# The first batch's keys arrive with the sequence along the free axis, and every engine's list is ordered anew

## The chip, the cores and the metric

The kernel runs on one core of a Trainium2 chip. The metric is the device time of one execution in microseconds (us). A core has five engines that each work through a list of their own: TensorE (PE: matmuls, with PEld for the loading of weights), VectorE (DVE), ScalarE (ACT), GpSimd (POOL) and SyncE (SP), which here issues every DMA. They wait for one another by semaphores. The shapes are fixed: batch 8, 8 heads, sequence 576, head dimension 64; 4608 tokens of width 512 and an FFN of width 2048.

## The reference

```
q_s = exp(q - max(q, over the 64 of a head));  q_s /= sum(q_s) + 1e-9
k_s = exp(k - max(k, over the 576 of the sequence));  k_s /= sum(k_s) + 1e-9
kv  = k_s^T v            (64 x 64 for each batch and head)
x   = q_s kv             -> tokens (4608) x model (512)
h   = x w_in;  g = h * sigmoid(1.702 h);  out = g w_out
```

The softmax of the queries runs along the head dimension, that of the keys along the sequence. All is fp32.

## The kernel before

Tokens are taken in 12 blocks t of 384 (128 partitions x 3). The work falls into a start (attention of the first blocks while the weights stream in), the FFN of blocks 0 and 1 straight from the freshly converted weights, and the FFN of the other ten blocks by a scheme of sums and products of quarter matrices (lines 1251, 1386 and 1514). The change touches the start.

**Keys of one batch** (`k_max` and `k_sub`, two groups i of four heads). `load_k` brings a group as 128 partitions x 4 heads x 5 chunks x 64: the partition is the position in the sequence, so the maximum over the sequence goes across chunks and partitions. VectorE takes maxima over chunks (lines 581, 584, 587), GpSimd reduces across the 128 partitions (line 591), VectorE subtracts the maximum (line 605), ScalarE takes the exponential of 1280 elements per partition (line 610). The last chunk has only 64 positions of its own; it is filled up with repeated ones, whose V rows count nothing through a zero in V's column of ones, which gives the sum.

**KV and x.** `kv_pairs` multiplies K by V for two pairs of heads (line 643, 40 short matmuls), VectorE divides by the sum (lines 651, 652, 661). The queries go through `q_soft` (lines 711 to 731), are transposed by TensorE (`q_tr`, line 753, three transposes for a pair of heads) and copied out by ScalarE (line 760). `x_pairs` multiplies them by KV (line 825), and `x_out` splits x into a high and a low half: ScalarE copies the high one (line 789), TensorE subtracts it in PSUM (line 799), ScalarE copies the rest (line 801).

**Weights.** `w_in` and `w_out` come as 64-bit words, wi and wo with a number j from 0 to 15 for a slice of 128 of the FFN's width; from 2 on two slices come together. `conv_w` turns them into a high and a low fp32r half in five steps: c1 on ScalarE (line 448), c2, a shift (line 452), and c3, a combination (line 456), on VectorE, c5, the cast to the high half, on ScalarE (line 463), c6, the low half, on VectorE (line 473).

**FFN of a block.** `g1` is 12 matmuls of 384 columns (line 853) with x and wi[j], then the activation and its two halves; `g2` three pieces of three matmuls of 512 columns (line 885) with wo[j].

**Dummy groups.** `warm` (line 1599) multiplies the identity by itself twice into a bank that nothing reads; a group shows as four matmuls in the trace. Ten groups are in the lists before.

**What sets the order.** Every step is added to a `Plan` with its engine, a cost, and what it reads and writes. Which step comes when is then fixed by the list FIRST: FIRST[n] is the place of the n-th step. A step starts on its engine only behind the step of that engine with the next lower place, so FIRST gives each engine its list; costs and ranks in the code no longer change it.

Of the kernel before, what the change touches and what calls it, by code (L numbers as in the profile page):

```python
# [11 lines left out]
U32 = mybir.dt.uint32  # L12
AF = mybir.ActivationFunctionType
# [4 lines left out]
class Plan:  # L18
# [95 lines left out]
LIMIT = 48  # L114
FIRST = [
# [177 lines left out]


@with_exitstack
def efficient_attention_then_gelu_ffn(
    ctx: ExitStack,
    tc: tile.TileContext,
    q: bass.AP,
    k: bass.AP,  # L300
    v: bass.AP,
    w_in: bass.AP,
    w_out: bass.AP,
    eye: bass.AP,
    out: bass.AP,
# [226 lines left out]
    def load_q(t, i, rank):  # L532
# [32 lines left out]
        )  # L565

    nm = [0]
    maxes, made = {}, {}

    def k_max(b, i, rank):  # L570
        n = group(b)
# [1287 lines left out]
```

## Time and profile before

| | us |
|---|---|
| median of 3 runs (lowest, highest) | 826.06 (825.77, 826.37) |
| the profiled execution | 825.61 |
| its span, first to last instruction | 823.8 |
| TensorE busy (share) | 807.6 (98%) |
| VectorE busy | 607.9 (74%) |
| ScalarE busy | 488.7 (59%) |
| GpSimd busy | 24.0 (3%) |

The span is measured between the first and the last instruction; the execution's own time has 1.8 us around it. A matmul's duration in the trace includes the time in which it runs through the array, so that successive ones overlap; the distance between their starts says what one costs.

### The profile page before, as it was taken

The page shows a single profiled execution, that of the slowest core. Times are in us where ns is not written, and L with a number is a line of the kernel's source. Part 1 is how long each engine was busy: PE and PEld are TensorE (multiplying, and loading weights), DVE is VectorE, ACT ScalarE, POOL GpSimd, SP SyncE. Part 2 cuts the span into 40 slices and gives each one's busy share as a digit, 9 for nine tenths or more (in the row PEclk, how much of TensorE's full clock was granted, in tenths as well). Part 3 has the DMA queues.
Part 4 walks back from the last instruction along what each step waited for, and adds up shares of the span by engine and source line. Part 5 has one row for each costly group of instructions (what it writes and reads, how often), then busy time and mean ns, then how long its engine had stood idle before and what let it go on. Part 6 is the DMA issues. An engine that isn't in the chain of part 4 may idle for free.

```text
span 823.8 us, 14925 instructions
## 1 busy us (share of the span) xinstructions
PE 807.6 (98%) x5740; PEld 758.9 (92%) x5740; DVE 607.9 (74%) x1091; ACT 488.7 (59%) x895; POOL 24.0 (3%) x21
## 2 busy tenths in 40 slices
PE   5899999999999999999999999999999999999998
PEld 5788998788888889999999999999999999999998
DVE  7999897588888876876787767788755677554374
ACT  3787647466546666755675664667475465444443
POOL 2101100010001000010000000000000000000000
PEclk8999999999999999999999999999999999999999
DMA  9998987438888989996887869686776768776772
GB/s 346 408 401 315 382 324 280 162 100 295 310 286 293 303 298 325 315 355 262 291 293 237 296 250 368 234 283 218 270 273 242 253 207 287 269 269 241 266 268 82
DMA packets 83190, 229.79 MB, mean 279 GB/s; under 512 B 8240, under 2 KB 32944, under 8 KB 83120
## 3 DMA queue, kind: packets, MB, share of 16 engines
q1 hardware_dynamic: 83120, 228.85, 78.6%
q8 instruction: 45, 0.74, 0.4%
q14 instruction: 25, 0.20, 0.1%
HBM read 181.63 MB, written 47.19 MB: 278 GB/s over the span
## 4 chain that ended last, share of the span: by engine, by line
PE 92%; DVE 6%; DMA 1%; issue 0%; SPq 0%; ACT 0%; DVEq 0%
PE bank L1251 35%; PE bank L1386 29%; PE bank L1514 8%; PE bank L885 7%; PE bank L853 7%; PE bank L825 2%; PE bank L643 2%; PE bank L753 2%; DVE work L456 1%; DMA dwb<-sl 1%; DMA eq<-in_q 1%; DVE w L473 1%; DVE kvn L661 1%; DVE raw L452 0%; DVE en L731 0%; DVE eq L715 0%
## 5 line engine op out<-in xcount | busy, mean ns | idle before, releaser
L1251 PE MATMUL bank<-xc,w 128*128 128x384 f32 x1680 | 312.6, 336 | 0.0
L1251 PEld LDWEIGHTS bank<-xc,w 128*128 128x128 f32 x1680 | 289.1, 188 | 3.6 <-ACT bank L1293 0.6
L1386 PE MATMUL bank<-w,pu 128*128 128x256 f32 x1260 | 167.5, 282 | 0.0
L1386 PEld LDWEIGHTS bank<-w,pu 128*128 128x128 f32 x1260 | 159.1, 189 | 3.9 <-issue 3.8
L1386 PE MATMUL bank<-w,xc 128*128 128x256 f32 x756 | 101.7, 281 | 0.0
L1386 PEld LDWEIGHTS bank<-w,xc 128*128 128x128 f32 x756 | 95.7, 188 | 1.4 <-issue 1.2
L853 PE MATMUL bank<-xh,w 128*128 128x384 f32 x256 | 70.7, 342 | 0.6 <-DVE w L473 0.6
L885 PE MATMUL bank<-w,gh 128*128 128x512 f32 x192 | 61.0, 399 | 0.0
L853 PEld LDWEIGHTS bank<-xh,w 128*128 128x128 f32 x256 | 47.3, 190 | 3.5 <-DVE w L473 0.9
L1270 DVE TENSOR_TENSOR g<-bank,g 128x384 f32<-128x384 f32 x33 | 18.4, 557 | 41.1 <-PE bank L1251 37.7
L1293 ACT COPY g<-bank 128x384 f32<-128x384 f32 x52 | 25.0, 481 | 32.3 <-PE bank L1251 30.1
L853 PE MATMUL bank<-xl,w 128*128 128x384 f32 x128 | 43.3, 338 | 0.0
L885 PEld LDWEIGHTS bank<-w,gh 128*128 128x128 f32 x192 | 34.9, 188 | 7.1 <-issue 1.5
L1293 ACT COPY bank<-bank 128x384 f32<-128x384 f32 x40 | 18.6, 465 | 37.0 <-PE bank L1251 37.0
L1278 ACT ACTIVATE g<-bank 128x384 f32<-128x384 f32 x51 | 25.0, 491 | 25.2 <-PE bank L1251 22.4
L885 PE MATMUL bank<-w,gl 128*128 128x512 f32 x96 | 37.8, 394 | 0.0
L591 POOL PARTITION_ALL_REDUCE mx<-mx x16 | 23.3, 1470 | 496.6 <-DVE mx L587 496.6
L1289 DVE TENSOR_TENSOR pu<-g,pu 128x384 fp32r<-128x384 f32 x47 | 25.7, 555 | 10.9 <-ACT pu L1286 10.4
L859 ACT ACTIVATE g<-bank 128x384 f32<-128x384 f32 x32 | 15.5, 490 | 29.8 <-PE bank L853 29.6
L760 ACT COPY qT<-bank 128x384 f32<-128x384 f32 x40 | 18.7, 482 | 18.8 <-PE bank L753 18.8
L1514 PE MATMUL bank<-w,gp 128*128 128x512 f32 x108 | 29.8, 395 | 0.0
L1270 DVE TENSOR_TENSOR work<-bank,work 128x384 f32<-128x384 f32 x16 | 8.9, 557 | 28.2 <-PE bank L1251 21.3
(187 smaller groups left out, 1320.9 us busy)
## 6 DMA issues: line engine op xcount, KB each, us to landing
w<-dwo SPq DMA_DIRECT2D x48, 512.0 KB, 5.6
w<-dwb SPq DMA_DIRECT2D x48, 512.0 KB, 6.0
w<-dwi SPq DMA_DIRECT2D x44, 512.0 KB, 5.4
w<-dsh SPq DMA_DIRECT2D x32, 512.0 KB, 5.7
w<-dsl SPq DMA_DIRECT2D x32, 512.0 KB, 6.1
w<-dwa SPq DMA_DIRECT2D x32, 512.0 KB, 5.3
vt<-in_v SPq DMA_DIRECT2D x14, 650.0 KB, 7.7
kt<-in_k SPq DMA_DIRECT2D x14, 640.0 KB, 6.9
```

What stands on the lines that cost most here:

```text
L591: nc.gpsimd.partition_all_reduce(flat, flat, P, bass_isa.ReduceOp.max)
L643: nc.tensor.matmul(pk[r0 : r0 + D, m // 2, m % 2], kt[:, o + a, c, :], vt[:, o + a, c, :], start=c == 0, stop=c == CM - 1, tile_position=( ...
L760: (nc.vector.tensor_copy if 4 <= t < 6 else nc.scalar.copy)(qT, pq[:, :TB])
L853: nc.tensor.matmul(ph, wi[w][j][:, c, :], x[:, c, :], start=c == 0 and i == 0, stop=c == KC - 1 and i == 2,)
L885: nc.tensor.matmul(po[c], x[:, cs], wo[w][j], start=j == 0 and i == 0, stop=j == NJ - 1 and i == 2)
L1251: nc.tensor.matmul(pb, ws[w][:, c * P : (c + 1) * P], xx[x][:, c * TB : (c + 1) * TB], start=p in FRESH and c == 0 and i == 0, stop=c == 1 ...
L1270: lambda: nc.vector.tensor_tensor(out=d, in0=pb, in1=o, op=ALU.add),
L1278: lambda: nc.scalar.activation(d, src, AF.Gelu_apprx_sigmoid), table="gelu")
L1289: lambda: nc.vector.tensor_tensor(out=get()[1], in0=d, in1=get()[0].bitcast(F32), op=ALU.subtract),
L1293: plan.add("ACT", act(TB), (PB,), (key,), free_, lambda: nc.scalar.copy(dst, pb))
L1386: nc.tensor.matmul(po, y[:, cs], w, start=start and i == 0, stop=i == 2, skip_group_check=True,)
L1514: nc.tensor.matmul(po[:, f0:f1], x[:, cs], w[:, h * DM + f0 : h * DM + f1], start=m == 0 and e == 0 and i == 0, stop=m == NQ - 1 and e == ...
```

## The change

1. The keys of batch 0 are handed over a second way, `k_t`: for each group 128 partitions x 2 x 640, where the partition is a pair of a head and a position in the head dimension, and the 640 are the sequence with its repeated positions. `k` keeps batches 1 to 7. The bytes of a load are the same. The tiles (`flip`) lie where block 1's x will be later.
2. For batch 0 `k_max` and `k_sub` are replaced by `k_turn`: VectorE takes the maximum along the free axis of 2 x 576 and negates it, ScalarE takes the exponential of each half (640) with that as its bias, TensorE transposes each half back in five 128x128 pieces, and ScalarE copies the result into the tile that `k_sub` would have filled: four pieces of a half in one copy of 512, the fifth pieces of both halves in one of 256.
3. There are 22 dummy groups in place of 10.
4. FIRST is new from end to end (3240 steps in place of 3222).
5. A constant column `floor` is set by VectorE, for a second form of c2 on ScalarE that `BYTES` would choose; `BYTES` is empty. The cost of c2 in the plan is a little higher.

```
+    def k_turn(i, rank):
+        rows = flip[i].rearrange("p (y s) -> p y s", y=2)
+        turned = [("x", 1, "hl"[i], y) for y in range(NP)]
+        t, key = kbuf[0, i]
+        tail = (2, 7)[i]
+        tops = peak[:, 2 * i : 2 * i + 2]
+        def run_m():
+            nc.vector.tensor_reduce(out=tops, in_=rows[:, :, :S], axis=AX.X, op=ALU.max)
+        def run_0():
+            nc.vector.tensor_scalar_mul(tops, tops, -1.0)
...
+        for y in range(2):
+            top, bk = peak[:, 2 * i + y : 2 * i + y + 1], 4 + y
+            def run_e(y=y, top=top):
+                nc.scalar.activation(rows[:, y], rows[:, y], AF.Exp, bias=top)
+            def run_t(y=y, bk=bk):
+                for c in range(CM):
+                    to = bank[bk][:, c * P : (c + 1) * P] if c < CM - 1 else bank[tail][:, y * P : (y + 1) * P]
+                    nc.tensor.transpose(to, rows[:, y, c * P : (c + 1) * P], ident)
+            def run_c(y=y, bk=bk):
+                to = t[:, 2 * y : 2 * y + 2, : CM - 1].rearrange("p a c d -> p c a d")
+                nc.scalar.copy(to, bank[bk].rearrange("p (c a d) -> p c a d", a=2, d=D))
...
+        def run_z():
+            nc.scalar.copy(t[:, :, CM - 1], bank[tail][:, : 2 * P].rearrange("p (h d) -> p h d", d=D))
...
     def attend(t, b, r, step):
         for i in range(2):
-            at(r, k_max, b, i)
-            at(r + step, k_sub, b, i)
+            if b == 0:
+                at(r, lambda rank, i=i: k_turn(i, rank))
+            else:
+                at(r, k_max, b, i)
+                at(r + step, k_sub, b, i)
...
-    for i in range(10):
+    for i in range(22):
         at(-89.05 + 0.001 * i, lambda rank: plan.add("PE", 0.93, ("ident",), (("bank", 3),), rank, warm))
```

What the two FIRST lists say, step by step, of the beginning of each engine's list (a number in brackets is a batch or block and a group or pair of heads; "max", "sub", "exp", "sum", "1/sum" and "norm" are steps of a softmax; c1 to c6 those of a weight):

```
SyncE before  q(0,1) eye q(0,0) k(0,0) k(0,1) wi0 k(1,0) wo0 v(0,0) v(0,1) wi2,3 wi1 k(1,1) v(1,0) q(1,0) wo1 ...
SyncE after   q(0,1) eye q(0,0) k(0,0) k(0,1) wo0 q(1,0) k(1,0) wi0 wi1 v(0,0) v(0,1) wi2,3 v(1,0) k(1,1) wo1 ...

TensorE before  6 dummies, q_tr(0,1) q_tr(0,0), 3 dummies, kv(0,0), q_tr(0,3), 1 dummy, q_tr(0,2), kv(0,1),
                x(0: 0,1) x(0: 2,3), 4 subtractions for x, kv(1,0), g1 wi0 wi1 wi2 wi3, q_tr(1,0) q_tr(1,1), g2 ...
TensorE after   8 dummies, turn(0) half 0, 2 dummies, turn(0) half 1, 5 dummies, q_tr(0,1), turn(1) halves 0 and 1,
                q_tr(0,0), 3 dummies, kv(0,0), 2 dummies, q_tr(0,3), 2 dummies, q_tr(0,2), kv(0,1),
                x(0: 0,1) x(0: 2,3), 3 subtractions, kv(1,0), 1 subtraction, q_tr(1,0) q_tr(1,1),
                g1 wi0 wi1 wi2, g2 two pieces, g1 wi3, g2 two pieces, x(1: 0,1), g2 two pieces, kv(1,1), g1 wi4 ...

VectorE after, from batch 0's keys on
  max and negation of k(0,0), max of k(0,1), sum q(0,1), negation of k(0,1), sum q(0,0), 1/sum, max q(1,0),
  norm q(0,0), three maxima of k(1,0), 1/sum q(0,1), c2 wo0, norm q(0,1), c2 wi0, c3 wo0, c3 wi0, sub k(1,0),
  sub q(1,0), sums of kv(0,0), c2 wi1, c6 wo0, kv(0,0) twice, sums of kv(0,1), kv(0,1) twice, c6 wi0, sum q(1,0),
  1/sum, c3 wi1, c2 wi2,3, norm q(1,0), c3 wi2,3, two maxima of k(1,1), c6 wi1, c6 wi2,3, max k(1,1), c2 wo1,
  c3 wo1, sums of kv(1,0), low half of g (block 0, j 0), sub k(1,1), kv(1,0), c6 wo1, low half of g (0, 1),
  max q(1,1), c2 wi4,5, kv(1,0), c3 wi4,5, c2 wo2,3, sub q(1,1), c3 wo2,3, c6 wi4,5 ...

ScalarE after
  exp q(0,1), exp q(0,0), exp k(0,0) half 0 and 1, exp k(0,1) half 1, two copies of turn(0), minus, exp k(0,1) half 0,
  c1 wo0, c1 wi0, last copy of turn(0), copy of turn(1), qT(0,0), two copies of turn(1), c1 wi1, c5 wi0, c5 wo0,
  exp k(1,0), qT(0,3) qT(0,2) qT(0,1), exp q(1,0), c1 wi2,3, the four high and four low halves of block 0's x,
  c5 wi1, c5 wi2,3, c1 wo1, activation of g (0, 0) ...
```

Behind these, the two lists hold the same steps in a similar order to the end; on TensorE, of 776 steps that both have apart from dummies and key transposes, none is more than 13 places from where it was.

## Rows read from the trace of the kernel before

**Rows 1.** Waits of TensorE over the whole span: engine, line, waited for, total, times, longest.

```profile
PE bank L753 <- DVE en L731: 4.4, 1, 4.4
...
PE bank L643 <- ACT ek L610: 2.5, 1, 2.5
PE bank L853 <- DVE w L473: 0.6, 1, 0.6
PE bank L753 <- ACT raw L777: 0.6, 1, 0.6
```

**Rows 2.** Windows: busy time and instructions of each engine, granted clock, DMA share, GB/s.

```profile
12.00:19.00 7.00, 5.40 (x44) 5.17 (x46) 6.90 (x10) 2.78 (x5) 3.42 (x2) 0.52 1.02 416
19.00:20.00 1.00, 1.00 (x24) 0.93 (x23) 0.88 (x3) 1.00 (x1) 0.00 (x0) 0.97 1.06 426
...
30.00:31.00 1.00, 1.00 (x16) 0.88 (x14) 1.00 (x3) 0.57 (x1) 0.00 (x0) 0.50 1.03 422
31.00:32.00 1.00, 1.00 (x4) 1.00 (x4) 0.96 (x2) 1.00 (x2) 0.00 (x0) 0.50 1.03 413
32.00:33.00 1.00, 1.00 (x6) 1.00 (x5) 1.00 (x2) 0.43 (x2) 0.00 (x0) 0.64 1.03 410
...
48.00:128.00 80.00, 79.46 (x417) 72.05 (x418) 71.63 (x103) 53.45 (x77) 5.40 (x2) 1.00 0.93 354
```

**Rows 3.** Timeline of TensorE's matmuls, 0 to 45 us: start, duration, instruction, count.

```profile
3.99 5.23 PE L1599 MATMUL bank<-ident 128*128 128x128 f32 x24 [3.99 <-DMA ident<-in_eye]
...
19.98 0.61 PE L1599 MATMUL bank<-ident 128*128 128x128 f32 x4
20.42 0.49 PE L753 MATMUL bank<-ident,en 128*128 128x128 f32 x3
...
30.69 0.69 PE L853 MATMUL bank<-xh,w 128*128 128x384 f32 x1
...
40.07 0.82 PE L753 MATMUL bank<-ident,en 128*128 128x128 f32 x6
40.64 0.70 PE L885 MATMUL bank<-w,gh 128*128 128x512 f32 x2
```

**Rows 4.** VectorE by line and form, 0 to 40 us: busy, mean ns, idle before.

```profile
L711 DVE TENSOR_REDUCE qm<-eq 128x12 f32<-128x768 f32 x4 | 3.7, 934 | 3.6 <-DMA eq<-in_q 3.6
...
L605 DVE TENSOR_TENSOR kt<-kt,mx 128x1280 f32<-128x1280 f32 x2 | 3.0, 1484 | 0.0
...
L456 DVE SCALAR_TENSOR_TENSOR work<-work,raw 128x512 int32<-128x512 int32 x4 | 2.7, 685 | 0.2
...
L584 DVE TENSOR_TENSOR mx<-tmp 128x256 f32<-128x256 f32 x4 | 1.6, 412 | 0.0
L452 DVE TENSOR_SCALAR raw<-raw 128x512 uint32<-128x512 uint32 x4 | 1.6, 425 | 0.0
...
L581 DVE TENSOR_TENSOR tmp<-kt 128x512 f32<-128x512 f32 x2 | 1.4, 680 | 0.0
...
L661 DVE TENSOR_TENSOR kvn<-bank,r 64x128 f32<-64x128 f32 x4 | 1.2, 288 | 0.1
...
L587 DVE TENSOR_TENSOR mx<-mx,kt 128x256 f32<-128x256 f32 x2 | 0.8, 392 | 0.0
```

**Rows 5.** Timeline of VectorE where batch 0's keys arrive.

```profile
8.31 0.68 DVE L581 TENSOR_TENSOR tmp<-kt 128x512 f32<-128x512 f32 x1
8.91 1.80 DVE L723 TENSOR_REDUCE qm<-eq 128x12 f32<-128x768 f32 x2
```

**Rows 6.** Timeline of ScalarE ahead of the first FFN matmul.

```profile
11.02 0.67 ACT L448 ACTIVATE work<-raw 128x512 f32<-128x512 f32 x1 [1.75 <-DMA raw<-in_w_in]
...
15.93 1.28 ACT L610 ACTIVATE kt<-kt 128x1280 f32<-128x1280 f32 x1
...
20.11 0.60 ACT L463 CAST w<-work 128x512 fp32r<-128x512 f32 x1
...
28.61 0.84 ACT L801 CAST xl<-bank 128x384 fp32r<-128x384 f32 x2
```

More of the change, by code (lines that the diff above doesn't have):

```diff
@@ L12 @@
 U32 = mybir.dt.uint32
+U8 = mybir.dt.uint8
 AF = mybir.ActivationFunctionType
@@ L114 @@
 LIMIT = 48
+BYTES = ()
 FIRST = [
[168 rows of a table removed]
[169 rows of a table added]
 ]
@@ L299, in efficient_attention_then_gelu_ffn @@
     q: bass.AP,
+    k_t: bass.AP,
     k: bass.AP,
@@ L341, in efficient_attention_then_gelu_ffn @@
     kvn = [sb(f"kvn{i}", [P, NP, P]) for i in range(2)]
-    xs = [[sb(f"x{s}{i}", [P, NP, TB], F32R) for s in "hl"] for i in range(2)]
+    flip = [sb(f"flip{i}", [P, 2 * CM * P], tag=f"x{s}1") for i, s in enumerate("hl")]
+    xs = {0: [sb(f"x{s}0", [P, NP, TB], F32R) for s in "hl"]}
     g = [sb(f"g{i}", [P, TB]) for i in range(4)]
@@ L354, in efficient_attention_then_gelu_ffn @@
     mx_ = [sb(f"mx{i}", [P, 4, D]) for i in range(2)]
+    floor = sb("floor", [P, 1])
+    nc.vector.memset(floor, -31.0 / 64.0)
     first = sb("first", [P, D])
@@ L438, in conv_w @@
         n = len(tags)
+        on_act = j in BYTES
         nwork[0] += 1
@@ L450, in c2 @@
         def c2():
+            if on_act:
+                top = raws[tags[0]].bitcast(U8)[:, :, :, 3]
+                nc.scalar.activation(words(0), top, AF.Identity, scale=2.0**-5, bias=floor)
+                return
             lo = words(0).bitcast(U32)
@@ L477, in conv_w @@
         plan.add("ACT", 0.23 + m / 1190, R, (T,), rank, c1)
-        plan.add("DVE", 0.13 + m / 1900, R, R, rank, c2)
+        plan.add("ACT" if on_act else "DVE", 0.23 + m / 1190 if on_act else 0.147 + m / 1900, R, R, rank, c2)
         plan.add("DVE", 0.147 + m / 960, (*R, T), (T,), rank, c3)
@@ L506, in load_k @@
     def load_k(b, i, rank):
+        if b == 0:
+            kbuf[b, i] = ek[b, i]
+            turned = tuple(("x", 1, "hl"[i], y) for y in range(NP))
+            plan.add(
+                "SP", plan.ISSUE, (), turned, rank,
+                lambda: nc.sync.dma_start(out=flip[i], in_=k_t[i]), size=P * 2 * CM * P * 4,
+            )
+            return
         t, key = kbuf[b, i] = ek[b, i] if b < 2 else (kt_[i], ("kt", i))
         def run():
-            nc.sync.dma_start(out=t.rearrange("p h c d -> p (h c d)"), in_=k[b, i])
+            nc.sync.dma_start(out=t.rearrange("p h c d -> p (h c d)"), in_=k[b - 1, i])
         plan.add("SP", plan.ISSUE, behind(b == 2), (key,), rank, run, size=P * 4 * CM * D * 4)
@@ L568, in efficient_attention_then_gelu_ffn @@
     maxes, made = {}, {}
+    peak = sb("peak", [P, NP])
+    def k_turn(i, rank):
[8 more added lines that the diff above has]
+            nc.vector.tensor_scalar_mul(tops, tops, -1.0)
+        T = ("peak", i)
+        plan.add("DVE", dve(2 * S), turned, (T,), rank, run_m)
+        plan.add("DVE", 0.17, (), (T,), rank, run_0)
+        for y in range(2):
[9 more added lines that the diff above has]
+                nc.scalar.copy(to, bank[bk].rearrange("p (c a d) -> p c a d", a=2, d=D))
+            plan.add("ACT", act(CM * P), (T, *turned), (("flip", i, y),), rank, run_e, table="exp")
+            plan.add("PE", 0.6, (("flip", i, y), *turned, "ident"), (("bank", bk), ("bank", tail)), rank, run_t)
+            plan.add("ACT", act(512), (("bank", bk),), ((*key, y),), rank, run_c)
+        def run_z():
+            nc.scalar.copy(t[:, :, CM - 1], bank[tail][:, : 2 * P].rearrange("p (h d) -> p h d", d=D))
+        plan.add("ACT", act(2 * P), (("bank", tail), (*key, 0), (*key, 1)), (key,), rank, run_z)
     def k_max(b, i, rank):
@@ L785, in x_out, with half @@
             return x_raw(t, hp, px, PB, rank)
-        xh, xl = (x[:, hp, :] for x in xs[t % 2])
+        def half(y):
+            if t % 2 not in xs:
+                xs[t % 2] = [sb(f"x{s}1", [P, NP, TB], F32R) for s in "hl"]
+            return xs[t % 2][y][:, hp, :]
         def run_h():
-            nc.scalar.copy(xh, px[:, :TB])
+            nc.scalar.copy(half(0), px[:, :TB])
         def run_l():
+            xh, xl = half(0), half(1)
             nc.vector.tensor_tensor(out=xl, in0=px[:, :TB], in1=xh.bitcast(F32), op=ALU.subtract)
@@ L798, in x_out @@
                 "PE", 0.36, ("minus", (*X, "h", hp)), (PB,), rank,
-                lambda: nc.tensor.matmul(px[:, :TB], minus_r, xh, start=False, stop=True, skip_group_check=True),
+                lambda: nc.tensor.matmul(px[:, :TB], minus_r, half(0), start=False, stop=True, skip_group_check=True),
             )
-            plan.add("ACT", act(TB), (PB,), ((*X, "l", hp),), rank, lambda: nc.scalar.copy(xl, px[:, :TB]))
+            plan.add("ACT", act(TB), (PB,), ((*X, "l", hp),), rank, lambda: nc.scalar.copy(half(1), px[:, :TB]))
             return
@@ L843, in g1 @@
         n = ng[0]
-        xh, xl = xs[t % 2]
         bk = 6 + n % 2
@@ L850, in run @@
         def run():
+            xh, xl = xs[t % 2]
             for c in range(KC):
@@ L1582, in attend @@
         for i in range(2):
-            at(r, k_max, b, i)
-            at(r + step, k_sub, b, i)
+            if b == 0:
+                at(r, lambda rank, i=i: k_turn(i, rank))
+            else:
+                at(r, k_max, b, i)
+                at(r + step, k_sub, b, i)
             at(r + step, lambda rank, t=t, i=i: q_soft(t, i, (rank, rank, rank)))
@@ L1825, in chunks @@
     def chunks(x):
-        y = x[:, :, order].reshape(B, G, 4, -1, P, x.shape[-1])
-        return np.ascontiguousarray(y.transpose(0, 1, 4, 2, 3, 5)).reshape(B, G, P, -1)
+        y = x[:, :, order].reshape(len(x), G, 4, -1, P, x.shape[-1])
+        return np.ascontiguousarray(y.transpose(0, 1, 4, 2, 3, 5)).reshape(len(x), G, P, -1)
+    flat = k[0][:, order].reshape(G, 2, 2, -1, D).transpose(0, 2, 4, 1, 3)
+    k_t = np.ascontiguousarray(flat).reshape(G, P, -1)
     wide = np.concatenate([v, np.ones_like(v[..., :1])], -1)
@@ L1836, in laid_out @@
     return {
-        "q": np.stack(qs), "k": chunks(k), "v": vs.reshape(B, G, P, -1), "w_in": ins.view(np.int64),
+        "q": np.stack(qs), "k_t": k_t, "k": chunks(k[1:]), "v": vs.reshape(B, G, P, -1), "w_in": ins.view(np.int64),
         "w_out": outs.view(np.int64), "eye": np.eye(P, dtype=np.float32),
```

337 rows, old and new, of the table FIRST are left out of this document.

## The prediction, made before the changed kernel was timed

> **What bounds the kernel now.** I read the waits of TensorE over the whole span first: after the start it waits for almost nothing [rows 1], the two longest waits (4.4 and 2.5 us) lie ahead of the first FFN matmul, and of those behind it the largest are 0.6 us each. The windows say the same: from 48 to 128 us TensorE is busy for 79.46 of 80 us [rows 2]. So the end is the start of the first FFN matmul, 30.69 us [rows 3], plus a list of matmuls that runs almost without a hole. Three things can be had: that start earlier; the half clock under the first FFN matmuls (granted clock 0.50 up to 32.72: a mean of 0.64 in 32 to 33 is 0.72 us at half [rows 2]); and the 0.6 us wait for a converted weight [rows 1]. What feeds the start is VectorE: busy for 6.90 of 7 us from 12 to 19 and 71.63 of 80 later [rows 2]. A microsecond taken off its list ahead of the first FFN matmul is a microsecond there, if no other engine comes last.
>
> **The change, part by part.** *VectorE loses*, per group of batch 0's keys, the three maxima (0.68, 0.41, 0.39) and the subtraction (1.48), 2.96 us [rows 4], 5.9 us for two, and the wait for GpSimd's reduction across partitions between them. *It gains* per group a maximum along the free axis of 2x576 elements and a negation of two. The first is not in the trace; the same operation on 768 elements takes 0.934 [rows 4], the nearest wider one 1.48 on 1280. Between the 512 and 1280 rows an element costs 1.05 ns, so 0.934 + 384 x 1.05 ns = 1.34; ends 0.93 and 1.48, value 1.34, because it is the same operation. With 0.2 for the negation, 3.1 us for two groups: 2.8 less.
>
> *ScalarE* swaps two exponentials of 1280 (1.28 each [rows 6]) for four of 640 (0.64 to 0.84 each; I take 0.7) and gains four copies of 512 (0.60 as the cast of that size [rows 6]) and two of 256 (0.4): 2.56 becomes 6.0, 3.4 more. A bias read per partition is not in the trace; I put it inside these ends and cost it at nothing more. The Trainium skill (ScalarE: Activation LUTs, What ACT_TABLE_LOAD costs) adds about 93 ns for each such operand. No run here shows it; four of them would be 0.37 us on ScalarE's list and would make the sum below 2.6.
>
> *TensorE* gains 20 transposes and 12 dummy groups. A transpose of 128 columns costs 0.095 (six from 40.07 to 40.64 [rows 3]), at half clock at most 0.22, the pitch of the dummies at 3.99. A dummy group is four matmuls: 0.87 at half clock (24 in 5.23), 0.44 at full (19.98 to 20.42) [rows 3]. All 22 stand ahead of the first FFN matmul.
>
> *SyncE.* wi0's load goes from the sixth place to the ninth. It lands at 11.02 now [rows 6]; behind 1.57 MB more at 416 GB/s [rows 2] it lands at 14.8, wi1 at 16.1, V's groups at 17.7 and 19.3, about 2 us later than now. All are awaited later than that (below). The `floor` memset runs while VectorE waits for queries; BYTES is empty.
>
> **The new order, followed with these rows.** VectorE's list is fixed by the numbers. It reaches batch 0's keys at about 8.35, as now (8.31 [rows 5]). From there to the end of the softmax of batch 1's first query group, which two transposes ahead of the first FFN matmul now need, stand 39 instructions: two reductions 2.7, two negations 0.3, eight of 768 elements 7.6 (0.95 each), six small ones 1.2, batch 1's first key maximum and subtraction 2.96, eight conversion steps of 512 (three of 0.42, three of 0.685, two of 0.68) 4.7, four normalisations of KV (0.29) and their four small steps 1.9, one shift of 1024 0.7: 22.0 us [rows 4]. Independent neighbours overlap by some 0.08 (0.68 long, the next begins 0.60 later [rows 5]); for two thirds of them that takes off 1.9. So 8.35 + 20.1 = 28.5, with small waits 28.9. Two transposes: 29.5.
> ScalarE, from 9.95 (first key maximum and negation) to the last low half of x: four exponentials 2.8, six copies 3.2, c1 and casts of 512 (three of 0.67, two of 0.60) 3.2, one exponential of 1280 and one of 768 2.1, c1 of 1024 1.15, minus 0.3, twelve copies of 384 at 0.42 (two in 0.84 [rows 6]) 5.0: 17.8, with some 1.5 of waiting 29.3. Both lists end together; first FFN matmul at 29.7, **1.0 us earlier**.
> That these two are last and not TensorE needs the clock: from the first key transpose (10.7) to the first KV product 26 transposes and 10 dummy groups at full clock take 2.6 + 4.4 us and end at 17.7, when V lands.
>
> **The sum.** (1) First FFN matmul 1.0 earlier. (2) The two transposes that stood at 40.07 now stand before it: 0.57 [rows 3]. (3) TensorE has no idle stretch left over 1 us ahead of it, where the idle before batch 1's KV (2.5 [rows 1]) now lets the clock fall: 2.03 us at half clock become 1.0 at full, 1.0 saved. (4) Is VectorE 2.9 us earlier too? wi1's low half is four instructions behind the query group: 31.7, needed at 29.7 + 2.1 = 31.8. wi4's low half is 18 more, 12.7 us: 44.4; TensorE, four FFN products of 2.09, six 0.69 us pieces of the second layer, one x and one KV step later, wants it at 44.3. Margin nil at both, so I give back half of the 0.6 wait only: 0.3. Together 2.9. The profiled execution took 825.61 (span 823.8); less 2.9 is 822.7. The median of the runs is 0.45 above that execution: **823.1**.
> Behind 48 us nothing of the computation changes but the order. TensorE's list moves little (of 776 entries no one by more than 13 places) and there are only a few tenths to win [rows 1]; I put it at 0, bounds 0.9 better and 1.5 worse.
>
> **Rivals.**
> *Half clock at the first FFN matmul.* The stretch before it is short KV products, four subtractions by matmul and transposes, with waits on ScalarE between. For: after the KV of batch 1 and its idle, TensorE fell to 0.50 and did not rise before 32.72 [rows 2]. Against: the transposes and dummies around 20 us went at full clock [rows 3], and no such idle remains. Price: term 3 gone, 1.0, and a tenth for the transposes ahead of it, 824.2. The Trainium skill (TensorE: Matmul & The Clock Gate, Part 4: PE-mode transpose) speaks for it: transposes do not count as TensorE activity for the clock. By that rule the two transposes right before the FFN, and the 20 new ones, would not keep it up, and the time would be this rival's; the trace has no stretch of transposes alone to test it.
> *The gain comes back as weight waits.* VectorE and ScalarE are as full behind 30 us as before it and the margins in (4) are nil. If conversions keep the pace they have now, relative to time zero less the 2.8 us of list but with later loads and 3.4 us more on ScalarE, TensorE waits at wi1 and wi4 for what it won in (1) to (3): left are 0.5 us, 825.5. Against: the list of VectorE is really shorter, and ScalarE was busy for only 2.78 us of 12 to 19 [rows 2].
> *The dummies become the bound (slower).* Place: TensorE's own list from 10.7 to the second KV product. Today the clock rises only at 19.0 (0.52 from 12 to 19, 0.97 after [rows 2]), with TensorE at work since 13.6, and the dummies from 3.99 never left a pitch of 0.218 [rows 3]. If the clock stays at half beyond 10.7, each further microsecond costs half a microsecond of list, against a slack of 1.0 at the second KV product. So it decides from 18.5: (18.5 - 10.7)/2 - 1.0 = 2.9, all the gain. Rising at 22: 4.65 lost, 827.8; never before the FFN: about 10 lost, 833. Against: the first eight groups leave no idle behind 3.99, where today it idles from 9.2 to 13.6.
>
> **How the numbers follow.** About 0.2%, 1.65 us, can be told from no change: faster is below 824.4. Chances: the forecast 0.62 (its own range 821.6 to 824.5: the reduction's bounds +-0.4, transposes, the later order -0.9 to +1.5), half clock 0.12, weight waits 0.17, dummies 0.08, the rest 0.01. Faster: nearly all of the forecast and two thirds of the second, 0.69. Same: the weight waits with what is left of these, 0.22. Slower: the dummies and a bad later order, 0.09. The range for 8 in 10 reaches from 821.3 to 825.9: out are the dummies, half of the better tail and a part of the weight waits.
>
> **What would show it.** The first line-853 matmul at 29.0 to 30.4 and at a pitch of 0.17 from the first; granted clock 1.00 well before 18 us and up to there without a fall; the transposes of queries of batch 1 ahead of it; VectorE without idle from 8.4 to 29; no wait of TensorE over 0.6 behind 30 us; the reduction at 1.34. I am wrong in step 1 if the first FFN matmul starts behind 30.7, in step 3 if the clock row shows 0.50 under it, in step 4 if TensorE's waits for wi or wo between 30 and 60 exceed 1.5 us, and about the later order if TensorE's waits behind 60 us add up to more than 2.

## The result: 831.35 us, slower where faster was forecast

The changed kernel takes 831.35 us (median of 4 runs, 831.02 to 831.85) against 825.95 for the kernel before (4 runs): a ratio of 1.0065, interval 1.0053 to 1.0077. The forecast was 823.1. The profiled execution took 831.63 (span 829.9), 6.0 more than the one of before.

The start went mostly as forecast. The timeline of TensorE's matmuls in the changed kernel (start, duration, instruction, count) answers to [rows 3]:

```profile
3.91 5.29 PE L1671 MATMUL bank<-ident 128*128 128x128 f32 x32 [3.91 <-DMA ident<-in_eye]
11.45 0.77 PE L619 MATMUL bank<-ident,flip 128*128 128x128 f32 x5 [2.24 <-ACT flip L614]
...
29.78 0.88 PE L817 MATMUL bank<-ident,en 128*128 128x128 f32 x6
30.41 0.42 PE L922 MATMUL bank<-xh,w 128*128 128x384 f32 x1
30.67 0.34 PE L922 MATMUL bank<-xl,w 128*128 128x384 f32 x1
```

The first FFN matmul (line 922) begins at 30.41 instead of 30.69, behind the six query transposes that stood at 40.07, and the next one follows 0.26 later, not at half clock. The windows of the changed kernel (busy time and instructions of PE, PEld, DVE, ACT and POOL, granted clock, DMA share, GB/s) say the same of the clock, where [rows 2] had 0.52, 0.50 and 0.64:

```profile
12.00:19.00 7.00, 7.00 (x63) 6.81 (x61) 6.83 (x14) 5.97 (x14) 1.27 (x1) 1.00 1.02 415
19.00:20.00 1.00, 1.00 (x35) 1.00 (x36) 1.00 (x4) 0.61 (x2) 0.00 (x0) 1.00 1.05 410
30.00:31.00 1.00, 1.00 (x9) 1.00 (x8) 1.00 (x2) 1.00 (x3) 0.00 (x0) 1.00 1.06 425
32.00:33.00 1.00, 1.00 (x8) 1.00 (x7) 1.00 (x2) 0.98 (x2) 0.00 (x0) 1.00 1.02 397
48.00:128.00 80.00, 80.00 (x416) 71.95 (x415) 72.90 (x105) 55.05 (x75) 2.71 (x2) 1.00 0.93 352
```

So the loss is later. To see where, I compare the time at which TensorE has done equally much work in the two traces (its list counted in columns, dummies and key transposes left out). Changed less before, by the time of the kernel before:

```
at us     60     180    200    300    342    500    700    787    808    end
       -2.33   -2.18  -0.91  -0.90  +0.15  +1.49  +3.55  +4.05  +5.77  +6.00
```

There are three steps (near 195, 332 and 793 us) and one slope (342 to 787, 3.9 us without any wait). The steps are in the waits of TensorE of the changed kernel, whole span (line, waited for, total, times, longest), as in [rows 1]:

```profile
PE bank L619 <- ACT flip L614: 2.2, 1, 2.2
PE bank L1455 <- DMA w<-dwa: 1.4, 1, 1.4
PE bank L817 <- ACT raw L841: 1.3, 2, 0.7
PE bank L1320 <- DVE g L1339: 1.0, 1, 1.0
```

Its timeline names the places. At 196.67 a product waits for VectorE, which itself has just waited 2.08 for a reloaded weight; at 333.58 a transpose of queries waits for ScalarE, and at 795.11 a product for a load:

```profile
196.67 0.61 PE L1320 MATMUL bank<-xc,w 128*128 128x384 f32 x2 [0.99 <-DVE g L1339]
...
333.58 0.55 PE L817 MATMUL bank<-ident,qt 128*128 128x128 f32 x3 [0.74 <-ACT raw L841]
...
795.11 2.06 PE L1455 MATMUL bank<-w,pu 128*128 128x256 f32 x15 [1.42 <-DMA w<-dwa]
```

```profile
195.46 0.69 DVE L1065 TENSOR_TENSOR sl<-w 128x512 f32<-128x512 f32 x1 [2.08 <-DMA w<-dwo]
```

The slope is no wait. In the windows (TensorE alone) both kernels are busy for all of it at full clock, but the changed one gets fewer matmuls through. Before, then changed:

```profile
340.00:560.00 220.00, 219.19 (x1708) 1.00 0.82 288
560.00:785.00 225.00, 225.00 (x1666) 1.00 0.73 251
```

```profile
340.00:560.00 220.00, 219.14 (x1697) 1.00 0.80 281
560.00:785.00 225.00, 225.00 (x1650) 1.00 0.74 255
```

And here are the same 36 matmuls of 384 columns in both timelines, before and changed; from the start of one row to the start of the next they take 6.25 us (173.6 ns each) and 6.33 us (175.8 ns each):

```profile
645.98 6.41 PE L1251 MATMUL bank<-xc,w 128*128 128x384 f32 x36
652.23 1.22 PE L1386 MATMUL bank<-w,xc 128*128 128x256 f32 x9
```

```profile
648.93 6.49 PE L1320 MATMUL bank<-xc,w 128*128 128x384 f32 x36
655.26 1.24 PE L1455 MATMUL bank<-w,xc 128*128 128x256 f32 x9
```

Below, *pitch* is the mean distance from the start of one matmul to the start of the next inside such rows, from 340 to 785 us; distances with a pause in them (over 150 ns for 256 columns, over 200 for 384) and those under 100 and 150 ns are left out. It is 118.1 ns (256 columns) and 174.1 (384) before, 119.6 and 175.5 changed. With some 1550 and 1150 such distances that is 1550 x 1.4 ns + 1150 x 1.4 ns = 3.8 us, nearly the whole slope. (The expectations below were written with a coarser measure, which gives 117.8 where this one gives 118.1.)

### The profile page after: what moved, and what is told of

Read it like the earlier page. It is cut to its first block, busy times and chain, and to the rows that moved or that the text cites. A ratio compares the mean times of both kernels' runs of the same rounds, so it can differ in the third digit from the quotient of the medians.

```text
span 829.9 us, 15085 instructions
## 1 busy us (share of the span) xinstructions
PE 815.5 (98%) x5808; PEld 767.0 (92%) x5808; DVE 607.3 (73%) x1088; ACT 495.2 (60%) x907; POOL 17.8 (2%) x19
## 4 chain that ended last, share of the span: by engine, by line
PE 93%; DVE 2%; DMA 2%; ACT 1%; issue 0%; SPq 0%; ACTq 0%; DVEq 0%
PE bank L1320 35%; PE bank L1455 28%; PE bank L922 8%; PE bank L1583 8%; PE bank L954 8%; PE bank L894 2%; PE bank L707 2%; PE bank L817 2%; DMA w<-dwa 1%; DMA eq<-in_q 1%; DMA w<-dwo 1%; DVE peak L602 0%; ACT ek L674 0%; DVE qm L775 0%; DVE qm L787 0%
## 5 line engine op out<-in xcount | busy, mean ns | idle before, releaser
L1455 PE MATMUL bank<-w,xc 128*128 128x256 f32 x756 | 103.4, 283 | 0.0
L1362 ACT COPY bank<-bank 128x384 f32<-128x384 f32 x40 | 18.5, 463 | 42.8 <-PE bank L1320 35.6
L1358 DVE TENSOR_TENSOR xc<-g,xc 128x384 fp32r<-128x384 f32 x32 | 17.6, 554 | 14.1 <-ACT xc L1355 12.3
L1355 ACT CAST pu<-g 128x384 fp32r<-128x384 f32 x47 | 24.0, 514 | 6.6 <-DVE g L1369 3.7
```

The source lines that it names most:

```text
L1355: plan.add("ACT", act(TB), (dk, *after), (*hk, *fresh, *gate), early_, lambda: nc.scalar.copy(get()[0], d))
L1358: lambda: nc.vector.tensor_tensor(out=get()[1], in0=d, in1=get()[0].bitcast(F32), op=ALU.subtract),
L1362: plan.add("ACT", act(TB), (PB,), (key,), free_, lambda: nc.scalar.copy(dst, pb))
L1455: nc.tensor.matmul(po, y[:, cs], w, start=start and i == 0, stop=i == 2, skip_group_check=True,)
```

## The experiments

Two suspects for the slope: the order, and the places of tiles in SBUF. SBUF is the core's on-chip memory. `sb` makes a tile there; tiles of one tag share a place, and the places are given one behind the other as tags are first used. The change makes two new small tiles, `floor` (which takes 32 bytes, ahead of the weight tiles) and `peak` (32 bytes, in their midst), and `flip` takes the place of a block's x first. In the compiled kernels eighteen weight tags lie in two sets: eight tiles of two weights that have a double role (wo6 to wo15 and wi10 to wi15; queries of both batches, keys and values of batch 1, and later all of `pu` and more than half of `xc` lie there too), here *the eight*, and behind `peak`, r and qm ten others (wi0 to wi9, wo0 to wo5; the rest of `xc`), *the ten*. Bytes past a multiple of 128:

```
                     the eight   the ten
before                   64          0
changed                  96         64      (floor moves the eight by 32, floor and peak the ten by 64)
```

**Order or tiles.** Four kernels. Under "measured" each median is followed by its ratio to the kernel before, timed beside it, and by the 95% interval of that ratio.

```
e1_aligned (from the changed kernel)
-    floor = sb("floor", [P, 1])
-    nc.vector.memset(floor, -31.0 / 64.0)
-    peak = sb("peak", [P, NP])
+    peak = sb("peak", [P, 16])[:, :NP]
e2_floor_alone (from the kernel before)
+    floor = sb("floor", [P, 1])
+    nc.vector.memset(floor, -31.0 / 64.0)
e3_new_start_old_rest: e1 with FIRST new to TensorE's 96th step, old behind it
e4_old_start_new_rest: the kernel before with FIRST old to TensorE's 80th step, new behind it
```

> The changed kernel with its order untouched, but without the unused floor column; peak takes 64 bytes instead of 32, so that every tile behind it starts at a multiple of 64 bytes, as in the kernel before. In the changed kernel 10 tiles of weights begin 32 bytes off. Placement theory (the drift behind 200 us, about 0.2 us per 20 us and some 4.6 us in all, is the price of operands 32 bytes off a multiple of 64 for the matmuls): the 256-column matmuls of line 1455 return from a pitch of 0.120 to 0.118, and the time falls from 831.4 to 826.0 to 827.5. Order theory (the new lists make TensorE wait a little at many places): the time stays at 831.4, within 1.

> The kernel before with nothing but the floor column and its memset put in at the place that it has in the changed kernel: order and work are those of before, but every weight tile behind it begins 32 bytes off a multiple of 64. Placement theory: slower by 4 to 7 us, 830 to 833, as a longer pitch of the matmuls spread over the FFN, with no new wait. Order theory: 826.0, no difference.

> The changed kernel with all tiles at multiples of 64 bytes, whose lists follow the new order up to the 96th step of TensorE (some 75 us) and the old order behind it. If the start is worth what the two traces show (TensorE 2.2 us ahead from 60 to 180 us) and the rest loses by placement and order alone: 823.3 to 824.3, faster than before. If an earlier start is given back by itself later (weights or transfers not earlier): 825.5 to 826.5. If the order of the start and not placement makes the drift: 828 to 830.

> The kernel before (old keys, 10 dummy groups, all tiles at multiples of 64 bytes) whose lists follow the old order up to its 80th step of TensorE and the new order behind it: the later order by itself. Placement theory with three stalls of the new order (0.9 at 195, 1.1 at 332, 1.7 at 793 us): 828.5 to 830. Order theory (the new lists cost all of the 8 us lost behind 180 us): 833 to 835. If the stalls too come from placement: 826.

Measured: e1 828.84 (1.0037, 1.0025 to 1.005), e2 827.00 (1.0011, 1.0002 to 1.002), e3 828.71 (1.0032, 1.002 to 1.0045), e4 827.97 (1.0026, 1.0016 to 1.0037). No single culprit: the column costs about 1 us by itself, and taking it out of the changed kernel, with `peak` widened to 64 bytes, mends 2.5 of 5.4. The placement theory missed in both: in the changed kernel it is the eight, and not ten tiles, that begin 32 bytes off a multiple of 64, and in e2 all eighteen do, at a pitch of 118.1 and 174.2. The later order costs too: e4 has the old code and the old pitch (118.1 and 174.1), and its trace loses 3.7 us from 60 us to its end, most of it at the same three places. That trace is of the slowest of e4's seven runs (830.08); by the medians e4 loses 2.2. But e3, with the old order behind 100 us, keeps a slope of 2.6 us from 342 to 787 (pitch 118.9 and 175.2), and e1 one of 2.8. That part belongs neither to the later order nor to the column. These four do not exclude that the order of the start makes it, which is e3's third expectation (828 to 830; 828.71 came); e11 below does. e3 also loses 2.1 where the two orders meet (TensorE waits 1.3 for a low half of g, which VectorE's old list has later).

**Which tiles.** e5 swaps the x tiles' places in the kernel before; e6 puts them back in e1. e7 and e8 ride on e6.

```
e5_swapped_alone (from the kernel before)
-    xs = [[sb(f"x{s}{i}", [P, NP, TB], F32R) for s in "hl"] for i in range(2)]
+    xs = {i: [sb(f"x{s}{i}", [P, NP, TB], F32R) for s in "hl"] for i in (1, 0)}
e6_old_places (from e1): flip is made behind xs[0], not ahead of it
e7_ten_dummies (from e6)
-    for i in range(22):
+    for i in range(10):
e8_old_rest (from e6): FIRST new to TensorE's 96th step, old behind it
```

> The kernel before with one edit: the four tiles of xs are made in the other order, so batch 0's keys (and raw0, raw1 on them) lie where batch 1's lay and batch 1's (and tt, sl on them) where batch 0's lay. Theory A (the longer pitch of the 256- and 384-column matmuls behind 340 us, 1.0 and 1.2 ns each, comes with these swapped places): pitch of the 256-column ones 118.9 instead of 117.8, some 2.7 us more, 828.5. Rival B (it comes with the tiles behind the small column, which lie 64 bytes further up in the changed kernel): 825.8, pitch 117.8. Rival C (it comes with something else in the changed code, such as the keys' chain): 825.8 too.

> The changed kernel with its tiles on multiples of 64 bytes, as in e1_aligned (828.8), and the four x tiles back at the places of the kernel before; the order and all else as changed. Theory A (swapped places): the pitch goes back to 117.8, the drift of 2.7 us between 340 and 790 us goes, 826.1, about the time before, with the late stalls left. Rival B (64 bytes further up behind the column, which this kernel still has) and rival C (other code): 828.8, pitch 118.9.

> e6_old_places with 10 dummy groups in place of 22 (8 and 2, where the order has them first). If the dummies hold the clock (step 3 of the prediction): a stretch at half clock comes back in the start, at the first FFN matmuls or ahead of them, and the kernel is 1 to 2 us above e6_old_places. Rival: the turns and other work ahead keep the clock up anyway, and it is within 0.3 us of e6_old_places.

> e6_old_places with the new order only to TensorE's 96th step, about 100 us, and behind it the order before. Theory A, with the later order's stalls at 195, 332 and 793 us costing what they showed: the start's 2.4 to 3.2 us stay, a seam where the two orders meet takes some 2, and the time is 824.5 to 825.5. Rivals B and C (the pitch is not of the x tiles' places): 828.7, as e3_new_start_old_rest.

Measured: e5 826.16 (0.9997, 0.9989 to 1.0006), pitch as before; e6 829.26 (1.0034, 1.0022 to 1.0045), pitch 119.0; e8 828.78 (1.003, 1.002 to 1.0041). My theory A, the swapped places, is dead from both sides. e7 is 829.21 (1.0034, 1.0021 to 1.0048), no different from e6. Its windows show a clock at half for part of the way, from 12 to 20 us:

```profile
12.00:19.00 7.00, 4.78 (x32) 4.21 (x32) 6.83 (x15) 4.74 (x10) 1.27 (x1) 0.80 1.02 417
19.00:20.00 1.00, 1.00 (x26) 1.00 (x28) 1.00 (x4) 1.00 (x3) 0.00 (x0) 0.66 1.04 414
20.00:26.00 6.00, 4.43 (x81) 3.15 (x78) 5.77 (x14) 5.80 (x10) 0.00 (x0) 1.00 1.02 410
```

but 1.00 from there on. Its first FFN matmul stands at 30.35, e6's at 29.63. That is not the price of the dummies: the first maximum of batch 0's keys began at 8.81 in e7, where VectorE waited for their load, and at 8.13 in e6, and in both traces the first FFN matmul follows it by 21.5 us.

```profile
8.81 1.35 DVE L593 TENSOR_REDUCE peak<-flip 128x2 f32<-128x1152 f32 x1 [0.79 <-DMA flip<-in_k_t]
```

**The 64 bytes.** e10 adds them to the kernel before; e11, e12 and e13 start from e6.

```
e10_shift64 (from the kernel before)
+    sb("pad", [P, 16])
     rs = [sb(f"r{i}", [P, NP]) for i in range(2)]
e11_no_shift (from e6)
-    peak = sb("peak", [P, 16])[:, :NP]
+    small = sb("small", [P, 4 * NP])
+    peak = small[:, 2 * NP : 3 * NP]
...
-    rs = [sb(f"r{i}", [P, NP]) for i in range(2)]
+    rs = [small[:, i * NP : (i + 1) * NP] for i in range(2)]
e12_old_weight_order (from e6), behind qm:
+    for tag, n in (("wi0", 1), ("wo0", 1), ("wi2", 2), ("wi1", 1), ("wo1", 1),
+                   ("wo2", 2), ("wi4", 2), ("wo4", 2), ("wi8", 2), ("wi6", 2)):
+        sb("hold", [P, n, DM, 2], I32, tag=tag)
e13_all_old_places: both
```

> The kernel before with one edit: an unused tile of 64 bytes ahead of r0, so that everything behind it (the ten weight tiles that have no double role) lies 64 bytes further up, as in the changed kernel. Theory B (the longer pitch comes with this shift): 256-column matmuls of 340 to 785 us at 118.9 ns instead of 117.8, 828.5. Rival D (it comes with which of the ten places each of these weight tiles has: their first loads come in another order in the changed kernel, and the place goes with that order) and rival C (other code of the change): 825.9, 117.8.

> e6_old_places (829.3) with peak, r0 and r1 packed in one tile of 64 bytes, so that nothing behind them is shifted. Theory B: pitch back at 117.8, 826.3. Rivals D and C: 829.3, 118.9.

> e6_old_places (829.3), still 64 bytes up, with the ten weight tiles claimed ahead in the order of the kernel before, so each stands where it stood there. Theory D: pitch back at 117.8, 826.3. Theory B and rival C: 829.3, 118.9.

> e11_no_shift and e12_old_weight_order together: the changed kernel, in its own order, with every tile that the kernel before has at the place that it has there. Theories B and D: 826.3, pitch 117.8, TensorE 2.4 to 3.2 us ahead at 180 us and the stalls of the later order behind. Rival C: 829.3, pitch 118.9.

Measured: e10 829.30 (1.0046, 1.0033 to 1.0058), e11 826.12 (1.0002, 0.9991 to 1.0012), e12 828.79 (1.0039, 1.0023 to 1.0054), e13 826.54 (1.0007, 0.9996 to 1.0017). An unused tile of 64 bytes makes the old kernel 3.5 us slower, and taking the shift out of the changed one makes it 3.1 faster. Theory B holds both ways; D and C fall, and so does the order of the start, which e11 keeps at a pitch of 118.1 and 174.1. The windows of e10 (TensorE alone) show the matmuls missing that the changed kernel misses, and its timeline has the same 36 matmuls at 6.31 us, 175.3 ns each:

```profile
340.00:560.00 220.00, 219.19 (x1699) 1.00 0.81 286
560.00:785.00 225.00, 225.00 (x1655) 1.00 0.72 252
```

```profile
648.52 6.47 PE L1252 MATMUL bank<-xc,w 128*128 128x384 f32 x36
654.83 1.23 PE L1387 MATMUL bank<-w,xc 128*128 128x256 f32 x9
```

**Own place or distance, and the sum of it all.**

```
e14_best: e13 with FIRST new through TensorE's 143rd real step, old behind it
e15_all_128 (from the kernel before): rs and qm are made ahead of first, not behind
e16_64_then_0 (from the kernel before)
+    sb("pad", [P, 16])
     first = sb("first", [P, D])
```

> All tiles at the places of the kernel before (as in e13_all_old_places), the new order through TensorE's 143rd real step, cut where both orders have done all but four of the same steps, the old order behind it. If the account is complete (start 2.4 to 3.2 us ahead, later order's stalls at 195, 332 and 793 us, longer pitch by the tiles' places): 822.6 to 823.5, with TensorE still some 3 us ahead at the end. Rival (the start's gain is given back by any order behind it): 825.8.

> The kernel before with the six small tiles (r, qm) made ahead of first, so that the eight double tiles behind it move up from 64 to 0 past a multiple of 128 bytes, while the ten other weight tiles stay at 0. Absolute theory (a weight tile at 64 past a multiple of 128 costs): pitch at 340 to 785 us no longer than 117.8 (256 columns) and 174.0 (384), 823 to 825.8. Relative theory (what costs is that both sets of tiles lie in the same half of 128 bytes, as in e10_shift64, where both were at 64): 118.9 and 175.1, 829.

> The kernel before with an unused tile of 64 bytes ahead of first: the eight double tiles move from 64 to 0 past a multiple of 128, the ten behind from 0 to 64. Absolute theory with the ten as the ones that matter: 118.9, 829. Relative theory (the two sets lie in different halves, as in the kernel before): 117.8, 825.9.

Measured: e14 823.55 (0.9974, 0.9965 to 0.9984), e15 828.36 (1.003, 1.0019 to 1.0042), e16 825.65 (0.9995, 0.9986 to 1.0003). With e10, the changed kernel and e2 (places alone differ in all but the changed kernel; e2 sets its column as well):

```
            the eight  the ten  apart   time    pitch 256   pitch 384
before          64        0      64    825.95     118.1       174.1
e16              0       64      64    825.65     118.2       174.2
e2              96       32      64    827.0      118.1       174.2
e15              0        0       0    828.36     119.1       174.1
e10             64       64       0    829.3      118.9       175.3
changed         96       64      32    831.35     119.6       175.5
```

The 256-column pitch goes by the distance of the two sets, not by either's own place: 118.1 to 118.2 at 64 bytes apart, in all eight kernels that have it (e4, e5, e11, e13 and e14 too), 118.9 to 119.1 at 0, in all eight (e1, e3, e6, e7, e8 and e12 too), 119.6 at 32. e16 is the plainest case: the shift of the ten that cost e10 3.5 us costs nothing once the eight move as well; its 36 matmuls are back at 6.25 us:

```profile
645.20 6.41 PE L1252 MATMUL bank<-xc,w 128*128 128x384 f32 x36
651.45 1.22 PE L1387 MATMUL bank<-w,xc 128*128 128x256 f32 x9
```

The relative theory is only half right for the 384 columns: e15 kept 174.1 where it expected 175.1.

The same traces show which matmuls pay. A matmul here reads two operands: `w` in 256 columns with 128 of `pu` or `xc` (`bank<-w,pu` and `bank<-w,xc`), or `xc` in 384 columns with 128 of `w` (`bank<-xc,w`). The trace has these matmuls in the order of the compiled list, which has each operand's address; sorted by the sets in which their two operands lie, the pitch is:

```
                                        before    e16     e2    e15    e10  changed
the sets apart                              64     64     64      0      0      32
256: w in the ten, other in the eight    117.3  117.3  117.4  119.3  118.6   120.0   (765 distances)
256: both in the eight                   119.1  119.2  119.1  119.0  119.3   119.3   (about 560)
256: both in the ten                     118.6  118.7  118.7  119.0  118.9   118.8   (191)
384: xc in the eight, w in the ten       174.2  174.2  174.2  174.0  176.1   175.9   (about 660)
384: both in the ten                     174.0  174.1  174.1  174.1  174.1   174.9   (about 483)
```

Matmuls with both operands in one set change by 0.9 ns at most; those with one in each carry the difference, 765 x 2.7 ns + 660 x 1.7 ns = 3.2 of the changed kernel's 3.9 us of slope. So the price goes with the places of a matmul's own two operands relative to each other, for 256 columns with their distance. Why e15 spares the 384 columns, and what it is in the memory, stays open. The Trainium skill (SBUF — State Buffer, Operand start alignment) gives a start address as a matter of what is legal, and its runs timed nothing; all places here are legal by it, and here they have a price. Open is also e2's 1 us with a good late pitch: its trace is 0.5 behind at 60 us and 0.9 from 600 on.

e14 has the new start, the old order behind it and the old places, and is faster than both kernels. Its lead over the kernel before is 2.99 at 60 us, 2.84 at 342, 3.02 at 787 and 2.34 at the end. Behind 100 us TensorE waits for little:

```profile
PE bank L811 <- ACT raw L835: 0.6, 1, 0.6
PE bank L1449 <- DMA w<-dwo: 0.4, 1, 0.4
PE bank L811 <- DVE raw L833: 0.3, 1, 0.3
```

The account in medians: start -2.4 (e14 against before), later order +3.0 (e13 against e14), places of tiles +4.8 (changed against e13, which also leaves out the column's memset), together +5.4. The three add up by the way they are taken, so the sum is no test; of the 4.8 the slope's 3.9 is the part that the pitch explains.

## Why the prediction was wrong

*Step 1 held, but small in this trace.* First FFN matmul at 30.41 for 29.7, so 0.3 earlier than before and not 1.0. In this execution the queries came late (VectorE idles 1.46 ahead of 7.12 for them), and the keys' maximum began at 8.98, not at 8.35; that is nearly the 0.7. In all ten traces with the new start the first FFN matmul follows that maximum by 21.4 to 21.6 us, and in e6 it stands at 29.63. The sizes behind it were right: the maximum of 2x576 took 1.35 (1.34 forecast), the exponential of 640 0.83 and two in a row 1.55 (0.7 each), a copy of 512 0.59, of 256 0.37. The first two lines are VectorE's, the others ScalarE's timeline:

```profile
7.12 0.95 DVE L775 TENSOR_REDUCE qm<-eq 128x12 f32<-128x768 f32 x1 [1.46 <-DMA eq<-in_q]
...
8.98 1.35 DVE L602 TENSOR_REDUCE peak<-flip 128x2 f32<-128x1152 f32 x1
```

```profile
10.57 1.55 ACT L614 ACTIVATE flip<-flip,peak 128x640 f32<-128x640 f32 x2 [0.62 <-DVE peak L605]
12.75 0.83 ACT L614 ACTIVATE flip<-flip,peak 128x640 f32<-128x640 f32 x1 [0.64 <-DVE peak L605]
```

Half of the 1.28 of an exponential of 1280 [rows 6] is 0.64; 0.83 is 0.19 more. Some of that is a part that does not go with the size: the copies of 512 and 256 (0.59 and 0.37) leave 0.15 at size nothing, an estimate. The Trainium skill (ScalarE: Activation LUTs, What ACT_TABLE_LOAD costs) put about 93 ns on a bias per partition; these rows leave room for it, and no run here takes it apart.

*Steps 2 and 3 held.* The transposes moved, and the clock was 1.00 at every FFN matmul. The first rival (half clock, 824.2) didn't come; the rule that speaks for it, in the Trainium skill (TensorE: Matmul & The Clock Gate, Part 4: PE-mode transpose), was not put to a test, since the clock had risen ahead of 12 us and dummies and real matmuls stand between the transposes. e7 shows that the clock under the FFN does not need the twelve added dummies. The dummies as the bound (827.8 or 833) didn't come either: the clock was up at 12 us, not at 18.5. That rival rested on a misreading. In the kernel before the clock did not rise only at 19.0, and its dummies did leave the pitch of 0.213: the last of the 24 comes 0.11 behind the one ahead of it, the granted clock is 1.00 from 9 to 12 us, and it falls to 0.50 at about 12.2, in TensorE's idle from 9.2 to 13.6. What the changed kernel has instead is an idle of 2.24 us ahead of 11.45, and there the clock stayed at 1.00; in e7, where TensorE also idles 2.22 us ahead of 15.72, the granted clock of 12 to 19 us is 0.80.

*Step 4 held.* From 30 to 60 us TensorE waits for nothing of 0.2 us or more, and the weight waits (825.5) did not come there. Steps 1 to 4 add up to 2.3 at 60 us in the changed kernel, 2.6 in e11 and 3.0 in e13 and e14, for 2.9 forecast.

*The step that failed* is the last: "Behind 48 us nothing of the computation changes but the order", put at 0 with bounds 0.9 better and 1.5 worse. It failed twice, and either failure alone is over its bound of 1.5. The order was mis-sized: I judged it by how far TensorE's entries move, 13 places at most, and by the waits of the kernel before, and neither bounds what a new order can add. It cost 3.0 us (e13 against e14). The stalls come from loads, VectorE and ScalarE steps around TensorE's list; the prediction's own sign of being wrong about the later order (waits behind 60 us over 2) came, with 1.4, 1.3, 1.0 and 0.2. And something else did change: I followed the `floor` memset as an instruction that runs where VectorE waits, but neither `floor` nor `peak` as a tile that takes room. They move eighteen weight tags, a cost that the prediction put at nothing without a reason; the places of the tiles cost 4.8 us (changed against e13), and the matmuls of 256 and of 384 columns from 340 to 785 us each took 1.4 ns longer in the mean.

## What to carry to other kernels

When a trace loses time without waiting, divide a row's time by its count: a pitch 1% longer at full clock was no matter of the schedule here. In a pool like this one any new tile, however small, moves the tiles that are allocated after it; before judging a change in a full SBUF, hold the old addresses (pack the small tile into an existing one, claim tags in the old order) or the comparison measures the move. And a new order is worth trying in parts: a cut where both orders have done nearly the same steps kept the half that wins (e14), and one elsewhere cost 2.1 at the seam (e3).

## What the hardware showed

- An unused tile of 64 bytes cost 3.5 us of 826 (e10), and one that shifts both sets as far cost nothing (e16). The pitch of the 256-column matmuls was 118.1, 118.9 to 119.1 or 119.6 ns by the distance of the two sets of tiles (64, 0 or 32 bytes), and the difference sits in those with one operand in each set. 512-column ones from 200 to 330 us, by the same measure, stood at 231.8 before, 232.2 in e10, 232.4 in the changed kernel and 230.2 in e16.
- The 32 dummy matmuls of the first stretch took 5.29 us where 24 took 5.23 [rows 3]: the distance between two falls from 0.213 to 0.112 us at about 7.0 us in the changed kernel, and only with the last one, at about 9.0, in the kernel before.
- The late stalls vary: behind 787 us e12's trace loses 0.6 us and e6's 3.9, with the same order in both; the one trace is of the fastest and the other of the slowest run of its kernel.
